# One attention-plus-FFN kernel: the first tiles in another written order, softplus halves side by side once the weights are converted, a chunk's scales computed earlier

## The chip, the cores and the metric

The kernel runs on one core of one Trainium2 chip, in one launch. The metric is the time of an execution in device microseconds (us). It was run three times: median 1319.87 us, lowest 1319.84, highest 1323.7.

## The reference

Two stages follow one another. The first is attention with a threshold, for 8 batches, 8 heads, 576 rows and a head size of 64; the second is a feed-forward network (FFN) with softplus over the 4608 rows that the first gives, 512 wide, with a hidden size of 2048. All inputs are given in 32 bits or more (the two weight matrices come in 64 bits).

```python
scores = scale * np.matmul(q, k.transpose(0, 1, 3, 2))
thresh = np.max(scores, axis=-1, keepdims=True) - tau
scores = np.where(scores >= thresh, scores, -1000000000.0)
attn = np.exp(scores - np.max(scores, axis=-1, keepdims=True))
attn = attn / (np.sum(attn, axis=-1, keepdims=True) + 1e-09)
x = np.matmul(attn, v)           # heads side by side: 4608 x 512
h = x @ w_in                     # 4608 x 2048
g = np.maximum(h, 0.0) + np.log1p(np.exp(-np.abs(h)))
out = g @ w_out                  # 4608 x 512
```

## The kernel before

**Units and tiles.** A unit is one pair of heads of one batch; there are 32. A unit has nine tiles of 128 score rows by 576 columns, so there are 288 tiles in one long row, and the main loop (L1003) goes over them. For tile g the loop writes out, step by step: the row maximum of tile g+2 (`row_max`, VectorE, tile `negm`), its exponentials (`exps`, ScalarE, tile `e_all`, and the threshold `thr`), the mask of tile g+1 (`mask`, VectorE: scores not below the threshold keep their exponential), the f16 high half of the weights of tile g+1 (`weights_hi` L560, GpSimd, tile `h`), the low half of tile g (`weights_lo` L566, VectorE, reads `e_all` and the high half), transposes, some of the FFN's matmuls, and the scores of tile g+3 (`scores` L465, TensorE, tile `s`). There are two PSUM buffers for scores (`banks`, L462): a tile's scores can only be written after the mask two tiles before has read its own. The first five units (`whole`) skip the split in halves and use 32-bit products.

**Halves.** TensorE gets 16-bit operands: a number is split in an f16 high half and an f16 rest. `halves` (L179) does it on GpSimd with two instructions, a conversion (TENSOR_SCALAR) and a subtraction (TENSOR_TENSOR).

**The FFN.** It runs between the tiles, in ten chunks (L893) of 512 or 256 rows. A chunk has 16 blocks `fc` of the hidden size. `hidden` (L699) makes the matmuls of a block into tile `h`, and two blocks at a time (`PAIR`) go through `softplus` (L721): ScalarE writes `st`, then scales it, and its inner function `parts` (L736) has `parts_of` (L747) split each of the two `st` into the halves `g`, with `halves` on GpSimd. `project` (L763) then multiplies `g` by `w_out` into tile `o`, in four quarters `qt` of four blocks for each 128 rows `tb`; `project_out` scales `o` into `acc` on VectorE. At the end of a chunk (`order`, L815) the last pair of blocks waits: `parts` puts itself into `waits` and is let go in the middle of a projection (L779).

**A chunk's scales.** `x_scale` (L654) makes `sx` (two small VectorE instructions) at the last projection ahead of the last quarter of the chunk before (L858). `h_scales` (L665: c0, c1, c2, three instructions of 128x4) and `o_scales` (L676: c3, one) are called from `hidden` (L703) and `project` (L775) at their first use. They are tiles of four numbers a partition.

**What sets the order.** The code is written out once and a scheduler places the instructions; each engine then runs its own queue in order. `defer(n, f)` puts f off by n points (`point`, L877; two points per tile, and the calls at the start), `force` and `need` bring deferred work forward. VectorE, ScalarE and GpSimd instructions go through `Queue` (L149): from tile TQ = 36 on each is tied behind the one written before it, so that these engines run in exactly the written order. Before tile 36 the scheduler is free. `prep` is the list of the weight pieces still to be read and converted, one for every two tiles (L913), 32 in all; it is empty after tile 62.

**The start** (L973 to L1000). Unit 0 is loaded, its K and Q are split (`split_k`, `split_q`: conversion on ScalarE, rest on VectorE for unit 0, on GpSimd for the others) and transposed (`qkT`), all of it for both heads j = 0 and 1, and only then come the scores, row maxima and exponentials of tiles 0 and 1. `queries` (L433) makes for unit 0 a second, swapped copy of the transposed Q with two VectorE instructions (`q` for j = 0, `qT` for j = 1). `plan` (L955) names the tile at which `top_v` (L372, the largest |v| of a unit: `vtop` on VectorE, then a small matmul `topv`) is written.

Of the kernel before, what the change touches and what calls it, by code (L numbers as in the profile page):

```python
# [55 lines left out]
PAIR = 2  # L56
NST = 4
TQ = 36
W1 = 2.0
W0 = 0  # L60
LATE = 4
# [4 lines left out]
def tile_kernel(ctx: ExitStack, tc: tile.TileContext, q, k, v, tau, w_in, w_out, out):  # L66
# [73 lines left out]
    now = {"p": 0, "tile": 0}  # L140
    masked = []

    def behind(i, others):

        if others:
            tc.add_manual_dep(i.ins, others[-1].ins.name, mybir.DependencyInfo(
                mybir.DependencyClass.NoSync, mybir.DependencyReason.DATA), reason="order")

    class Queue:  # L149
# [4 lines left out]
        def __getattr__(self, name):  # L154
            def call(*args, **kwargs):
                i = getattr(self.eng, name)(*args, **kwargs)  # L156
                if now["tile"] >= TQ:
                    behind(i, self.last)
                    self.last = [i]
                return i  # L160
            return call
# [186 lines left out]
    def load_q(s):  # L348
        s.qn = natural(s, q, "qn")
# [13 lines left out]
    def load_v(s):  # L363
        s.vn = apool.tile([P, 10, D], F32, tag="vt" if s.whole else "vn", bufs=2 if s.whole else 1, name=f"vn_{s.i}")
        load_rows(s, s.vn, v)
        for i in range(2):
            nc.sync.dma_start(
                s.vn.rearrange("p (h s) d -> p h s d", h=2)[i * SR:(i + 1) * SR, :, NC, :],
                v[s.b, 2 * s.hp:2 * s.hp + 2, SM:S, :].rearrange("h p d -> p h d"),
            )  # L370
# [29 lines left out]
    def split_q(s, j):  # L400
        t = apool.tile([P, NC + 1, 2 * D], F32R, tag="q2", bufs=1, name=f"q2_{s.i}_{j}")
        z = NC + 1 - j
        qj = s.qn[:, j * (NC + 1):j * (NC + 1) + z, :]
        hi_of(s.eng, t[:, 0:z, 0:D], qj)
        lo_of(s.eng_lo, t[:, 0:z, D:2 * D], qj, t[:, 0:z, 0:D])
        s.q2.append(t)
# [58 lines left out]
    def scores(s, t):  # L465
        if t == 0:
            s.sums = apool.tile([P, 9], F32, tag="sums", name=f"sums_{s.i}")
            s.e, s.sp, s.m, s.e16, s.eT = {}, {}, {}, {}, {}
        sp = banks[nth[0] % SB]
        s.e[t] = e_all[:, nth[0] % EB, :]  # L470
        nth[0] += 1
        s.sp[t] = sp
        if t == M:
            parts = [(qm[:, n, j, :], j) for j in range(2) for n in range(2)]
        else:
            j, c = divmod(t, NC + 1)
            parts = [(s.qT[j][n][:, c * P:(c + 1) * P], j) for n in range(2)]
        for m, (lhs, j) in enumerate(parts):
            for hf in range(2):
                nc.tensor.matmul(sp[:, hf, 0:HS], lhs, s.kT[j][:, hf * HS:(hf + 1) * HS],  # L480
                                 start=(m == 0), stop=(m == len(parts) - 1))

    def row_max(s, t):
        negm = apool.tile([P, 1], F32, tag="negm", bufs=3, name=f"negm_{s.i}_{t}")
        thr = apool.tile([P, 1], F32, tag="thr", bufs=3, name=f"thr_{s.i}_{t}")
        vec.reduce_max(negm, s.sp[t][:, :, 0:HS], axis=AX.XY, negate=True)
        s.m[t] = (negm, thr)
# [156 lines left out]
    def load_x(u, cc):  # L644

        if u.main:
            return
        for b in range(QB):
            need("q", NPAIR * (QB * u.b + b) + cc)
        st = fpool.tile([P, QB * SR], F32, tag="xst", name=f"xst_{u.n}_{cc}")  # L650
        u.st[cc] = st
        nc.sync.dma_start(st, x_d[u.b][:, cc, :])

    def x_scale(u):  # L654
        n = NPAIR * (1 if u.main else QB)
        for i in range(n):
            need("v", n * u.b + i)

        u.sx, u.px = [cpool.tile([P, 1], F32, tag=f"sx{i}", bufs=2, name=f"sx{i}_{u.n}") for i in range(2)]
        u.ch, u.g_top, u.sg, u.co = [cpool.tile([P, NFC // 4], F32, tag=f"c{i}", bufs=2, name=f"c{i}_{u.n}")  # L660
                                     for i in range(4)]
        vec.tensor_reduce(u.sx, v_scale[:, n * u.b:n * (u.b + 1)], axis=AX.X, op=ALU.min)
        inverse(u.px, u.sx)
# [57 lines left out]
    def softplus(u, full):  # L721


        ts, last_ = [], None
        with tc.high_priority(SPP):
            for fc, bank in reversed(full):
                t = fpool.tile([P, TC], F32, tag="st", bufs=NST, name=f"st_{u.n}_{fc}")
                i = act.activation(t, bank, AF.Softplus, scale=u.ch[:, fc // 4:fc // 4 + 1]).ins
                if last_ is not None:
                    tc.add_manual_dep(i, last_.name, mybir.DependencyInfo(  # L730
                        mybir.DependencyClass.NoSync, mybir.DependencyReason.DATA), reason="one table load")
                last_ = i
                ts.append((fc, t))
            for fc, t in reversed(ts):
                act.activation(t, t, AF.Copy, scale=u.sg[:, fc // 4:fc // 4 + 1])
        def parts():  # L736
            if u.n in waits:
                waits[u.n].append(parts)
                return
            for n, (fc, t) in enumerate(reversed(ts)):  # L740
                defer(n, lambda fc=fc, t=t: parts_of(u, fc, t))
        defer(HD[1], parts)

    waits = {}
# [2 lines left out]
    def parts_of(u, fc, t):  # L747

        home, tags, bufs = (fpool, ("gh", "gl"), NG)
        if u.tail:  # L750
            spare = [("kT", "kT", 2), ("qT0", "qT1", 1), ("nat", "nat", 2), ("vt", "vt", 2)]
            i = later_g[0] % (NG + len(spare))
            later_g[0] += 1
            if i >= NG:
                *tags, bufs = spare[i - NG]
                home = apool
        gh, gl = [home.tile([P, TC], F16, tag=tags[i], bufs=bufs, name=f"g{i}_{u.n}_{fc}") for i in range(2)]
        halves(gh, gl, t)
        for i in range(TC // u.T):
            c = slice(i * u.T, (i + 1) * u.T)  # L760
            u.g[fc + i] = (gh[:, c], gl[:, c])
# [49 lines left out]
    nq = NFC // QF  # L811
# [26 lines left out]
    def stream():  # L838
        for cc in range(len(X0), NCC):
            split_x(chunks[0], cc)  # L840
        for it in order():
            u = chunks[it[1]]
            if it[0] == "h":
                yield from hidden(u, it[2])
                continue
            if it[0] == "w":
                waits[u.n] = []
                continue
            if it[4] >= 0:

                nx = chunks[u.n + 1]
                per = NCC * P // u.T
                for cc in range(max(0, (it[4] - 1) * per), min(NCC, it[4] * per)):
                    split_x(nx, cc)
                    if cc + 2 < NCC:
                        load_x(nx, cc + 2)
                if it[4] == 0:
                    x_scale(nx)  # L858
                    load_x(nx, 0)
                    load_x(nx, 1)  # L860
            yield from project(u, it[2], it[3])
            if it[4] >= 0 and it[3] == u.T // P - 1 and (u.n, it[2], it[3]) not in early:
                for cc in range(it[4] * per, NCC):
                    split_x(nx, cc)
# [6 lines left out]
    def defer(n, f):  # L871
        if n == 0:
            f()
        else:
            later.append((now["p"] + n, f))

    def point():  # L877
        now["p"] += 1
        due = [x for x in later if x[0] <= now["p"]]
        later[:] = [x for x in later if x[0] > now["p"]]  # L880
        for _, f in due:
            f()
# [72 lines left out]
    plan = {}  # L955
    for s in units:
        if s.i == 0:
            times = ((0, -1), (0, 0))
        elif s.i == 1:
            times = ((0, -1), (0, 4))  # L960
        elif s.whole:
            times = ((s.i - 1, 4), (s.i - 1, 7))
        else:
            times = ((s.i - 1, 0), (s.i - 1, 3), (s.i - 1, 7))
        for at_, f in zip(times, (load_v, top_v, split_v)):
            plan.setdefault(at_, []).append(lambda f=f, s=s: f(s))
# [11 lines left out]
    eng, u0.eng, u0.eng_lo = u0.eng, act, vec  # L978
    split_k(u0)
    split_q(u0, 0)  # L980
    for n in (0, 2, 1):
        qkT(u0, 0, n)
        point()
    load_v(u0)
    load_k(units[1])
    load_q(units[1])
    split_q(u0, 1)
    for n in (0, 2, 1):
        qkT(u0, 1, n)
        point()  # L990
    u0.eng, u0.eng_lo = eng, pool
    scores(*tiles[0])
    row_max(*tiles[0])
    exps(*tiles[0])
    scores(*tiles[1])
    row_max(*tiles[1])
    exps(*tiles[1])
    mask(*tiles[0])
    scores(*tiles[2])
    load_v(units[1])  # L1000

    done = 0.0
# [81 lines left out]
```

## Time and profile before

The shares are of the span. A line of the profile names an engine, an operation and its operands as output<-inputs, with the buffer numbers left out; L156 stands for every instruction that goes through `Queue`. PE is TensorE's matmuls, PEld its weight loads, DVE is VectorE, ACT is ScalarE, POOL is GpSimd. All times are in us. "idle before <-releaser" is the time for which an engine stood still ahead of an instruction and what ended it.

| | |
|---|---|
| median of three runs | 1319.87 us |
| the profiled execution's own time | 1319.59 us |
| its span (first to last instruction) | 1317.8 us |
| TensorE busy | 1245.7 us (95%) |
| VectorE, ScalarE, GpSimd busy | 936.2, 907.2, 920.2 us |
| largest groups of matmuls | o 407.9, h 360.7 and 229.4, s 152.9 and 107.3, pv 153.6 us |
| mean granted TensorE clock | 0.994 |

Some 1.8 us of the execution lie outside the span.

### The profile page before, as it was taken

What the parts mean: (1) busy time and instruction counts of PE and PEld (TensorE: products, weight loads), DVE (VectorE), ACT (ScalarE), POOL (GpSimd) and SP (SyncE); (2) the same over time, 40 slices, a digit from 0 to 9 for tenths busy, and PEclk for the clock granted to TensorE, in tenths of its full rate; (3) what the DMA queues carried; (4) which work ended last, traced back from release to release, by engine and by line L of the source; (5) the groups of instructions that cost most, each with busy time, mean ns of one, the idle gap of its engine ahead of it and who ended that gap; (6) DMA issues with size and microseconds to landing.
All of it is one profiled execution on the core that took longest, in us unless ns stands there. A gap on an engine that the chain in (4) does not pass through costs nothing.

```text
span 1317.8 us, 21688 instructions
## 1 busy us (share of the span) xinstructions
PE 1245.7 (95%) x7153; PEld 752.0 (57%) x7153; DVE 936.2 (71%) x1738; ACT 907.2 (69%) x1715; POOL 920.2 (70%) x987
## 2 busy tenths in 40 slices
PE   5988988899999999998999899999999999999998
PEld 4655544455566566665666566655656755554455
DVE  5878888988878787888787877886677666640011
ACT  5877887886877677776777697768675867643321
POOL 2577788888777777778877786787666787564333
PEclk9999999999999999999999999999999999999999
DMA  4544458867876678787877787776667665530010
GB/s 127 159 139 126 125 129 165 180 112 149 160 149 146 139 161 152 150 148 161 149 143 145 161 149 142 145 150 132 130 125 163 115 132 114 98 78 17 1 40 17
DMA packets 395521, 168.79 MB, mean 128 GB/s; under 512 B 350448, under 2 KB 376464, under 8 KB 395408
## 3 DMA queue, kind: packets, MB, share of 16 engines
q1 hardware_dynamic: 395408, 167.40, 61.6%
q8 instruction: 57, 0.93, 0.3%
q14 instruction: 56, 0.46, 0.1%
HBM read 56.62 MB, written 10.63 MB: 51 GB/s over the span
## 4 chain that ended last, share of the span: by engine, by line
PE 57%; ACT 15%; POOL 12%; DVE 8%; issue 6%; DMA 2%; SPq 0%; POOLq 0%; ACTq 0%; DVEq 0%
PE o L776 20%; PE h L712 17%; PE s L480 9%; PE pv L591 6%; ACT L156 4%; ACT st L156 4%; POOL g L156 2%; ACT e_all L156 2%; DVE negm L156 2%; PE pv L550 2%; DVE e_all L156 2%; POOL xl L156 2%; PE tr L420 2%; POOL h L156 1%; POOL w_i L156 1%
## 5 line engine op out<-in xcount | busy, mean ns | idle before, releaser
L776 PE MATMUL o<-w_o,g 128*128 128x512 f16 x1728 | 407.9, 382 | 13.9 <-POOL g L156 11.0
L712 PE MATMUL h<-xh,w_i 128*128 128x512 f16 (+1 forms) x1280 | 360.7, 358 | 3.6 <-ACT kT L156 1.9
L156 POOL TENSOR_SCALAR h<-e_all 128x576 f16<-128x576 f32 x243 | 239.3, 985 | 121.5 <-DVE e_all L156 114.9
L156 ACT ACTIVATE e_all<-s,negm 128x576 f32<-128x576 f32 x288 | 213.8, 742 | 132.3 <-DVE negm L156 129.8
L712 PEld LDWEIGHTS <-w_i 128*128 128x128 f16 x1920 | 179.4, 98 | 165.9 <-issue 7.4
L776 PEld LDWEIGHTS <-g 128*128 128x128 f16 x1728 | 159.1, 98 | 191.4 <-POOL g L156 16.3
L156 DVE SCALAR_TENSOR_TENSOR e_all<-s,thr,e_all 128x576 f32<-128x576 f32 x288 | 233.0, 809 | 49.3 <-ACT thr L156 48.8
L156 DVE TENSOR_REDUCE negm<-s 128x1 f32<-128x576 f32 x288 | 215.2, 747 | 73.2 <-PE s L480 72.1
L156 DVE SCALAR_TENSOR_TENSOR h<-e_all,h 128x576 f16<-128x576 f32 x243 | 237.7, 978 | 2.5 <-POOL h L156 2.5
L712 PE MATMUL h<-xl,w_i 128*128 128x512 f16 (+1 forms) x640 | 229.4, 358 | 0.5 <-POOL xl L156 0.5
L156 POOL TENSOR_SCALAR g<-st 128x512 f16<-128x512 f32 x144 | 99.5, 691 | 165.1 <-ACT st L156 156.9
L156 DVE SCALAR_TENSOR_TENSOR acc<-o,c,acc 128x512 f32<-128x512 f32 x108 | 80.2, 743 | 171.8 <-PE o L776 110.6
L156 POOL TENSOR_TENSOR g<-st,g 128x512 f16<-128x512 f32 x144 | 171.2, 1189 | 12.0
L480 PE MATMUL s<-kT,q 128*128 128x288 f32 x768 | 152.9, 328 | 16.1 <-DVE e_all L156 13.6
L156 ACT ACT_TABLE_LOAD x119 | 152.7, 1283 | 3.9 <-DVE negm L156 1.9
L591 PE MATMUL pv<-eT,vt 128*128 128x288 f16 x1080 | 153.6, 288 | 1.2 <-DVE xp L156 0.4
L156 ACT ACTIVATE st<-h,c 128x512 f32<-128x512 f32 x144 | 91.2, 684 | 76.2 <-PE h L712 75.4
L480 PEld LDWEIGHTS s<-kT,q 128*128 128x128 f32 x768 | 115.0, 192 | 49.1 <-DVE e_all L156 35.6
L591 PEld LDWEIGHTS <-vt 128*128 128x128 f16 x1080 | 99.9, 98 | 37.9 <-issue 2.0
L480 PE MATMUL s<-kT,qT 128*128 128x288 f32 x512 | 107.3, 331 | 10.5 <-DVE e_all L156 8.7
L156 ACT COPY xp<-pv 64x288 f32<-64x288 f32 (+3 forms) x133 | 50.7, 385 | 87.1 <-PE pv L591 82.9
L156 ACT ACTIVATE st<-st,c 128x512 f32<-128x512 f32 x144 | 96.3, 716 | 2.3
(113 smaller groups left out, 1512.7 us busy)
## 6 DMA issues: line engine op xcount, KB each, us to landing
q<-q SPq DMA_DIRECT2D x62, 192.0 KB
kn<-in_k_dram SPq DMA_DIRECT2D x32, 256.0 KB
qn<-in_q_dram SPq DMA_DIRECT2D x32, 256.0 KB
vn<-in_v_dram SPq DMA_DIRECT2D x32, 256.0 KB
wc_i<-in_moe_w_in_dram SPq DMA_DIRECT2D x16, 512.0 KB
wc_o<-in_moe_w_out_dram SPq DMA_DIRECT2D x16, 512.0 KB
qT<-qT SPq DMA_DIRECT2D x62, 128.0 KB
out_dram<-acc SPq DMA_DIRECT2D x14, 512.0 KB
```

The costliest lines, as they stand in the source:

```text
L156: i = getattr(self.eng, name)(*args, **kwargs)
L420: nc.tensor.transpose(pr[:, c * P:(c + 1) * P], src, identr)
L480: nc.tensor.matmul(sp[:, hf, 0:HS], lhs, s.kT[j][:, hf * HS:(hf + 1) * HS], start=(m == 0), stop=(m == len(parts) - 1))
L550: nc.tensor.matmul(o[0:D, 0:n], s.vn[k_, 5 * j + c, :], h[k_, c, 0:n], start=(c == 0), stop=(c == NC))
L591: nc.tensor.matmul(o[:, 0:HS], s.vt[:, 5 * j + c, :], s.eT[j][:, c + i, x0:x0 + HS], start=(c == 0 and i == 0), stop=(c == NC and i > 0))
L712: nc.tensor.matmul(bank[:, i * u.T:(i + 1) * u.T], wi[g, cc][:, a, e], x[cc], start=(cc == 0 and m == 0), stop=(cc == NCC - 1 and m == 2))
L776: nc.tensor.matmul(o, u.g[fc][m // 2][:, sl], wo[fc][:, m % 2, :], start=(n == 0), stop=(n == 3 * QF - 1))
```

## The change

There are three parts.

1. **The start.** `Queue` now ties instructions in the written order for tiles 0 to 2 as well (TF = 3), and everything between tile 3 and tile 36 only behind the last of those. In the written order, the transposes of the first head come as n = 0, 1, 2, then the scores, row maxima and exponentials of tiles 0 and 1, and only then the second head's Q and its transposes, with the mask of tile 0 and the scores of tile 2 among them. The second head's Q of unit 0 is split on GpSimd instead of ScalarE and VectorE. `top_v` of units 0 and 1 is written at tiles 4 and 6 in place of 0 and 4.
2. **The halves of a pair.** In `parts`, the second block's halves were put off by one point. They are still put off while `prep` holds work; afterwards both blocks are split one right after the other.
3. **The scales.** `h_scales` and `o_scales` of the next chunk are called right after its `x_scale`.

```diff
--- before.py
+++ after.py
@@ -56,6 +56,7 @@
 PAIR = 2
 NST = 4
 TQ = 36
+TF = 3
 W1 = 2.0
 W0 = 0
 LATE = 4
@@ -154,8 +155,8 @@
         def __getattr__(self, name):
             def call(*args, **kwargs):
                 i = getattr(self.eng, name)(*args, **kwargs)
-                if now["tile"] >= TQ:
-                    behind(i, self.last)
+                behind(i, self.last)
+                if not TF <= now["tile"] < TQ:
                     self.last = [i]
                 return i
             return call
@@ -738,7 +739,7 @@
                 waits[u.n].append(parts)
                 return
             for n, (fc, t) in enumerate(reversed(ts)):
-                defer(n, lambda fc=fc, t=t: parts_of(u, fc, t))
+                defer(n if prep else 0, lambda fc=fc, t=t: parts_of(u, fc, t))
         defer(HD[1], parts)
 
     waits = {}
@@ -856,6 +857,10 @@
                         load_x(nx, cc + 2)
                 if it[4] == 0:
                     x_scale(nx)
+                    need("i", nq - 1)
+                    need("o", nq - 1)
+                    h_scales(nx, 0)
+                    o_scales(nx, 0)
                     load_x(nx, 0)
                     load_x(nx, 1)
             yield from project(u, it[2], it[3])
@@ -955,9 +960,9 @@
     plan = {}
     for s in units:
         if s.i == 0:
-            times = ((0, -1), (0, 0))
+            times = ((0, -1), (0, 4))
         elif s.i == 1:
-            times = ((0, -1), (0, 4))
+            times = ((0, -1), (0, 6))
         elif s.whole:
             times = ((s.i - 1, 4), (s.i - 1, 7))
         else:
@@ -978,25 +983,25 @@
     eng, u0.eng, u0.eng_lo = u0.eng, act, vec
     split_k(u0)
     split_q(u0, 0)
-    for n in (0, 2, 1):
+    for n in (0, 1, 2):
         qkT(u0, 0, n)
         point()
+    u0.eng, u0.eng_lo = eng, pool
     load_v(u0)
     load_k(units[1])
     load_q(units[1])
+    for g in range(2):
+        scores(*tiles[g])
+    for g in range(2):
+        row_max(*tiles[g])
+        exps(*tiles[g])
     split_q(u0, 1)
     for n in (0, 2, 1):
         qkT(u0, 1, n)
         point()
-    u0.eng, u0.eng_lo = eng, pool
-    scores(*tiles[0])
-    row_max(*tiles[0])
-    exps(*tiles[0])
-    scores(*tiles[1])
-    row_max(*tiles[1])
-    exps(*tiles[1])
-    mask(*tiles[0])
-    scores(*tiles[2])
+        if n == 0:
+            mask(*tiles[0])
+            scores(*tiles[2])
     load_v(units[1])
 
     done = 0.0
```

Part 2 on GpSimd, inside chunk 1. Its rows before: `g_1_4` and `g_1_5` are the two blocks of a pair (first the conversion, then the subtraction of each), `h` the high half of a tile's weights, `vt` the halves of v.

```order
L156 TENSOR_SCALAR g_1_4_4136<-st_4_4115 128x512
L156 TENSOR_TENSOR g_1_4_4137<-st_4_4115,g_1_4_4136 128x512
L156 TENSOR_SCALAR h_132<-e_all 128x576
L156 TENSOR_SCALAR g_1_5_4157<-st_5_4113 128x512
L156 TENSOR_TENSOR g_1_5_4158<-st_5_4113,g_1_5_4157 128x512
L156 TENSOR_SCALAR h_132<-e_all 128x576
L156 TENSOR_SCALAR vt_4213<-vn_3883 128x10x64
```

The same place after:

```order
L157 TENSOR_SCALAR g_1_4_4136<-st_4_4116 128x512
L157 TENSOR_TENSOR g_1_4_4137<-st_4_4116,g_1_4_4136 128x512
L157 TENSOR_SCALAR g_1_5_4140<-st_5_4114 128x512
L157 TENSOR_TENSOR g_1_5_4141<-st_5_4114,g_1_5_4140 128x512
L157 TENSOR_SCALAR h_132<-e_all 128x576 x2
L157 TENSOR_SCALAR vt_4213<-vn_3884 128x10x64
```

The conversion of a tile's weights that stood between the two blocks now stands behind them, next to the following tile's. This happens seven times in each of chunks 1 to 4; three of the seven (blocks 4/5, 8/9, 12/13) look like this one, with another `h` next; elsewhere a split of q follows.

Part 2 on GpSimd at the end of chunk 1, where the last pair (blocks 14 and 15) was held back. `xh` and `xl` are the halves of the next chunk's x. Before:

```order
L156 TENSOR_SCALAR g0_1_14_5206<-st_1_14_5173 128x512
L156 TENSOR_TENSOR g1_1_14_5207<-st_1_14_5173,g0_1_14_5206 128x512
L156 TENSOR_SCALAR h16_132<-e_all_129 128x576
L156 TENSOR_SCALAR xh_2_0_5226<-xp_8_3783 128x512
L156 TENSOR_TENSOR xl_2_0_5227<-xp_8_3783,xh_2_0_5226 128x512
L156 TENSOR_SCALAR g0_1_15_5233<-st_1_15_5171 128x512
L156 TENSOR_TENSOR g1_1_15_5234<-st_1_15_5171,g0_1_15_5233 128x512
```

After:

```order
L157 TENSOR_SCALAR g0_1_14_5210<-st_1_14_5177 128x512
L157 TENSOR_TENSOR g1_1_14_5211<-st_1_14_5177,g0_1_14_5210 128x512
L157 TENSOR_SCALAR g0_1_15_5214<-st_1_15_5175 128x512
L157 TENSOR_TENSOR g1_1_15_5215<-st_1_15_5175,g0_1_15_5214 128x512
L157 TENSOR_SCALAR h16_132<-e_all_129 128x576
L157 TENSOR_SCALAR xh_2_0_5234<-xp_8_3787 128x512
L157 TENSOR_TENSOR xl_2_0_5235<-xp_8_3787,xh_2_0_5234 128x512
```

Block 15's halves moved ahead of one `h` and of one x split.

Part 3 on VectorE, at the start of chunk 2. `c0`, `c1`, `c2` are the scales, `xp` takes an attention result out of PSUM, `acc` an FFN result. Before:

```order
L156 TENSOR_REDUCE negm_13_1_5439<-s_0_130 128x1
L156 SCALAR_TENSOR_TENSOR e_all_129,sums_13_5373<-s_1_131,thr_13_0_5400,e_all_129 128x576
L156 SCALAR_TENSOR_TENSOR h16_132<-e_all_129,h16_132 128x576
L156 TENSOR_SCALAR c0_2_5158<-p_i_91,sx1_2_5157 128x4
L156 TENSOR_SCALAR c1_2_5159<-c0_2_5158 128x4
L156 TENSOR_SCALAR c2_2_5160<-c1_2_5159 128x4
L156 TENSOR_TENSOR xp_12_5415<-pv_12_0_5416,xp_12_5415 64x288
L156 SCALAR_TENSOR_TENSOR acc_1_2_4290<-o_1_3_3_5389,c3_1_3528,acc_1_2_4290 128x512
```

After, in the place to which they moved, some 30 rows earlier; the rows above are the same without them:

```order
L157 SCALAR_TENSOR_TENSOR h16_132<-e_all_129,h16_132 128x576
L157 TENSOR_REDUCE sx0_2_5156<-v_scale_90 128x1
L157 TENSOR_SCALAR sx1_2_5157<-sx0_2_5156 128x1
L157 TENSOR_SCALAR c0_2_5158<-p_i_91,sx1_2_5157 128x4
L157 TENSOR_SCALAR c1_2_5159<-c0_2_5158 128x4
L157 TENSOR_SCALAR c2_2_5160<-c1_2_5159 128x4
L157 SCALAR_TENSOR_TENSOR c3_2_5161<-c1_2_5159,p_o_92 128x4
L157 TENSOR_REDUCE negm_12_5_5220<-s_1_131 128x1
```

All four now follow `sx`, ahead of a row maximum. TensorE's order is the same from the middle of chunk 0's last quarter to the end of chunk 5; it differs at the start and at those two chunk ends.

## The prediction

> **What bounds the kernel now.** I read the page first (TensorE is busy for 95% of the span, the others about 70%), then the windows, to see in which stage TensorE stands still. The columns are the window, its length, then busy us of PE, PEld, DVE, ACT and POOL (instructions in brackets), the granted clock, the DMA share and GB/s.
>
> ```profile
> 0.00:25.00 25.00, 11.39 (x53) 9.97 (x54) 13.26 (x27) 12.36 (x27) 6.70 (x15) 1.00 0.59 167
> 25.00:60.00 35.00, 34.28 (x211) 23.60 (x209) 31.16 (x65) 28.61 (x78) 16.09 (x19) 1.00 0.45 129
> 300.00:900.00 600.00, 583.05 (x3412) 355.52 (x3410) 480.40 (x879) 435.15 (x796) 455.71 (x489) 1.00 0.77 150
> ```
>
> TensorE idles 13.6 us in the first 25, under 1 us in the next 35, and 17 us in the 600 of the steady stage. In that stage it is the bound: an idle microsecond taken from it is a microsecond off the time, if nothing else takes its place. The waits of TensorE, with their total, count and longest, say what it stood still for:
>
> ```profile
> PE o L776 <- POOL g L156: 11.0, 12, 1.9
> PE tr L413 <- DVE xp L156: 4.3, 6, 1.2
> ```
>
> These two kinds stand at chunk ends and chunk starts, and parts 2 and 3 of the change move just the instructions that they wait for. The start is the third place.
>
> **Part 2, the gain at the chunk ends.** The end of chunk 2, first TensorE, then GpSimd (start, duration, engine, instruction, and in brackets the idle time before it with its releaser):
>
> ```profile
> 591.94 1.69 PE L776 MATMUL o<-w_o,g 128*128 128x512 f16 x7
> 595.53 0.82 PE L776 MATMUL o<-w_o,g 128*128 128x512 f16 x3 [1.91 <-POOL g L156]
> 596.77 0.60 PE L776 MATMUL o<-w_o,g 128*128 128x512 f16 x2 [0.42 <-POOL g L156]
> ```
>
> ```profile
> 588.87 1.17 POOL L156 TENSOR_TENSOR g<-st,g 128x512 f16<-128x512 f32 x1
> 590.00 0.68 POOL L156 TENSOR_SCALAR h<-e_all 128x576 f16<-128x576 f32 x1
> 592.65 0.62 POOL L156 TENSOR_SCALAR xh<-xp 128x512 f16<-128x512 f32 x1 [1.97 <-ACT xp L156]
> 594.86 0.62 POOL L156 TENSOR_SCALAR g<-st 128x512 f16<-128x512 f32 x1
> 595.56 1.15 POOL L156 TENSOR_TENSOR g<-st,g 128x512 f16<-128x512 f32 x1
> ```
>
> TensorE is out of operands at 591.94 + 1.69 = 593.6 and waits for the last block's conversion (594.86) and subtraction (595.56). These sit behind an h and an x split, and that split waits 1.97 for ScalarE. Written next to the first block, they start at 590.0 and end at 590.0 + 0.62 + 0.08 + 1.15 = 591.9, 1.7 us before TensorE needs them; the 1.97 of idle takes them in, so x is not late. Both waits go, 2.33 us here. The row of waits has all twelve of this kind at 11.0, and each is a last block, so I take 11.0. What is late next: the four score matmuls after it need a mask that stands ahead of the `weights_lo` of 592.74 (quoted below) on VectorE and so had ended by then, and the next projection's operands are long there. Nothing is seen to take the place.
>
> **Part 2, the cost between the tiles.** The same edit puts the conversion of a tile's weights behind a pair instead of between its blocks, 28 times in chunks 1 to 4. VectorE needs it for `weights_lo`. GpSimd, VectorE and TensorE at one of them:
>
> ```profile
> 396.86 0.67 POOL L156 TENSOR_SCALAR h<-e_all 128x576 f16<-128x576 f32 x1
> 398.20 1.16 POOL L156 TENSOR_TENSOR g<-st,g 128x512 f16<-128x512 f32 x1
> 399.33 1.17 POOL L156 TENSOR_SCALAR h<-e_all 128x576 f16<-128x576 f32 x1
> ```
>
> ```profile
> 399.04 0.93 DVE L156 SCALAR_TENSOR_TENSOR h<-e_all,h 128x576 f16<-128x576 f32 x1
> 400.01 0.76 DVE L156 TENSOR_REDUCE negm<-s 128x1 f32<-128x576 f32 x1
> 400.68 0.81 DVE L156 SCALAR_TENSOR_TENSOR e_all<-s,thr,e_all 128x576 f32<-128x576 f32 x1
> ```
>
> ```profile
> 401.58 0.87 PE L480 MATMUL s<-kT,q 128*128 128x288 f32 x4
> ```
>
> VectorE goes without a gap from `weights_lo` (399.04) over the row maximum to the mask, which ends at 401.49, and TensorE's scores follow 0.09 later. A `weights_lo` that ends later is thus paid by TensorE. After the change the h of 396.86 ends where the pair ends now, at 398.20 + 1.16 = 399.36, and the next h, whose mask is done, runs right behind it to about 400.03. How VectorE fares beside a running GpSimd conversion is seen at the chunk end, where `weights_lo` starts 0.09 after the xh of 592.65 above; the second row is one without company:
>
> ```profile
> 592.74 1.14 DVE L156 SCALAR_TENSOR_TENSOR h<-e_all,h 128x576 f16<-128x576 f32 x1
> 587.39 0.75 DVE L156 SCALAR_TENSOR_TENSOR h<-e_all,h 128x576 f16<-128x576 f32 x1
> ```
>
> It takes 1.14 in place of 0.75 and ends 593.88, 0.61 after xh's end (593.27). By that, `weights_lo` would end at 400.03 + 0.61 = 400.64 instead of 399.97: 0.67 later, less the 0.09 of slack, 0.58. I take 0.55 a place. It applies at the three places a chunk where another h follows the pair, 12 in chunks 1 to 4, so 6.6 us. Where a split of q follows I take nothing; that is an assumption, since those 16 places are not shown, and rival (c) prices its failure. One more place, in chunk 0, where a weight subtraction follows h, I put at 0.5, like the others. The bounds for a place are 0 (VectorE takes its turn before the second h) and 0.7.
>
> The Trainium skill speaks against this part of the change: "SBUF — State Buffer", section "Who interferes with whom", says that a VectorE instruction with two SBUF inputs contends with a GpSimd instruction that reads SBUF, and that whoever issues first keeps the shared port for its whole instruction. By it `weights_lo` would run its full 0.75 after 400.03, 0.81 late at 12 places, 9.7 us in place of 6.6, and the result would be about 1314. The pair of rows 592.65 and 592.74 agrees with the wait, but shows 0.61 and not 0.75 behind it.
>
> **Part 3, the scales.** At the start of chunk 3, VectorE, then TensorE, then VectorE at the place to which the scales move (end of chunk 2), and the group of c3:
>
> ```profile
> 611.79 0.63 DVE L156 TENSOR_SCALAR c<-p_i,sx 128x4 f32<-128x4 f32 x1
> ...
> 612.74 0.44 DVE L156 TENSOR_TENSOR xp<-pv,xp 64x288 f32<-64x288 f32 x1
> ```
>
> ```profile
> 613.24 0.28 PE L413 MATMUL tr<-identr,k 128*128 128x128 f32 x1 [1.10 <-DVE xp L156]
> ```
>
> ```profile
> 585.24 0.15 DVE L156 TENSOR_SCALAR sx<-sx 128x1 uint32<-128x1 uint32 x1
> 585.99 0.76 DVE L156 TENSOR_REDUCE negm<-s 128x1 f32<-128x576 f32 x1 [0.60 <-PE s L480]
> 586.66 0.81 DVE L156 SCALAR_TENSOR_TENSOR e_all<-s,thr,e_all 128x576 f32<-128x576 f32 x1
> ...
> L156 DVE SCALAR_TENSOR_TENSOR c<-c,p_o 128x4 f32<-128x4 f32 (+1 forms) x13 | 7.6, 587 | 0.0
> ```
>
> ```profile
> 589.52 0.88 PE L480 MATMUL s<-kT,qT 128*128 128x288 f32 x4
> ```
>
> A transpose of TensorE waits 1.10 for a PSUM buffer that xp frees, and the three scales ahead of xp take 612.74 - 611.79 = 0.95. Without them xp starts 0.95 sooner and 0.15 of the wait stays. Of the 4.3 us of such waits I take 3.8. In the new place the four cost 0.95 + 0.59 = 1.5, of which 0.6 fall in the idle time before the row maximum. The mask after it then ends near 588.4 instead of 587.5; the scores that need it start at 589.52, so this is hidden, by a margin of 1.1.
>
> **Part 1, the start.** VectorE and TensorE:
>
> ```profile
> 11.13 0.82 DVE L156 TENSOR_REDUCE vtop<-vn 128x1 f32<-128x640 f32 x1 [1.60 <-DMA vn<-in_v_dram]
> 11.97 1.51 DVE L156 TENSOR_SCALAR q<-tr,qscale 64x512 fp32r<-64x512 f32 x2
> ...
> 16.70 1.51 DVE L156 TENSOR_SCALAR qT<-tr,qscale 64x512 fp32r<-64x512 f32 x2 [0.45 <-ACT qT L156]
> 18.25 0.82 DVE L156 SCALAR_TENSOR_TENSOR e_all<-s,thr,e_all 128x576 f32<-128x576 f32 x1
> ...
> 18.99 0.81 DVE L156 SCALAR_TENSOR_TENSOR e_all<-s,thr,e_all 128x576 f32<-128x576 f32 x1
> ```
>
> ```profile
> 13.54 1.09 PE L480 MATMUL s<-kT,q 128*128 128x288 f32 x3 [2.02 <-DVE q L156]
> 19.13 1.33 PE L480 MATMUL s<-kT,q 128*128 128x288 f32 x4 [3.67 <-DVE e_all L156]
> ...
> 21.18 1.31 PE L480 MATMUL s<-kT,q 128*128 128x288 f32 x4
> ```
>
> The copy q (11.97) waits behind a vtop that waits for v's transfer; without it q can start sooner by the 1.60 of that wait or a little more, near 10.0 (an estimate), and tile 0's scores end some 1.5 us sooner. Tile 0's mask (18.25) then goes ahead of qT and ends, by my estimate, near 15.7, not 19.0. But qT's 1.51 and a row maximum of 0.76 now stand before tile 1's mask, and qT, whose operands come from the second head's split, is put at no earlier than 17.0 (an estimate: now it starts at 16.70, and its split is written later): that mask begins at 17.0 + 1.51 + 0.76 = 19.2, as it does now (18.99). Tile 3's scores wait for it and start at 20.0, not at 21.18. So the first 25 us give back 1.1 us of the 3.67 and 2.02. Against this, two vtop (0.82 each) and three weight conversions of ScalarE move into the window 25:60, where TensorE is busy 34.28 of 35 and VectorE 31.16; VectorE would be at 32.8 there. I take 1.0, and from -1 to +3 as bounds.
>
> **The sum.** 11.0 + 3.8 + 1.0 - 6.6 - 0.5 = 8.7 us. From the profiled execution's own 1319.59 that gives 1310.9; the median of the runs is 0.28 above it, hence 1311.
>
> **The rivals.**
>
> (a) The moved conversions cost nothing: VectorE gets its turn between two h, or TensorE makes up for it at the next scores. For it: the shared stretch now already holds `weights_lo` up (0.93 at 399.04). Against it: the two h run without a gap on GpSimd. Then the gain is 15.8 - 0.5 = 15.3 and the time 1304.6.
>
> (b) The time won at the chunk ends is lost again: VectorE's masks run nearly back to back after a chunk's end, and if they set the pace there, half of the 11.0 stays. Then 8.7 - 5.5 = 3.2, 1316.7, no change to speak of. Against it: in the 600 us of the steady stage VectorE is busy for 480.40, so it stands idle for a fifth of it, seven times as long as TensorE.
>
> (c) Slower: each of the 28 moved conversions holds VectorE up by 0.65, not only the 12, because a split of q that runs on GpSimd holds it just as an h does. 28 x 0.65 = 18.2 against 15.3 gives +2.9, 1322.8. It decides from 15.3 / 28 = 0.55 a place on. For it: the 0.61 row is a conversion of the same kind as a q split. Against it: the 28 places are then all without slack on VectorE, which is idle for a fifth of this stage.
>
> (d) The clock. Two windows, with the clock in the third column from the end:
>
> ```profile
> 400.00:500.00 100.00, 97.20 (x562) 59.10 (x561) 81.58 (x149) 69.44 (x128) 75.07 (x81) 0.98 0.71 150
> 500.00:600.00 100.00, 97.63 (x577) 59.62 (x576) 78.10 (x148) 72.39 (x135) 73.39 (x81) 1.00 0.80 147
> ```
>
> The first lost 2% of its clock, 2 us, and holds a chunk end; the second holds one too and lost none. If it was that wait, removing it gives 2 us more, 1309; I do not count on it. The Trainium skill, "TensorE: Matmul & The Clock Gate", section "Part 1: The HAM clock gate", has TensorE fall to half its clock after about 3.4 us of idling; no wait in these windows is as long.
>
> **How the numbers follow.** About 0.3%, 4 us, can be told from no change here. Chances: the forecast 0.54, with 1307 to 1315 as its own bounds; (a) 0.16; (b) 0.14; (c) 0.07; (d) 0.09. Faster by over 0.3%, below 1315.9: the forecast, (a) and (d), 0.79. Within: (b), 0.14. Slower: (c), 0.07. The range from 1303 to 1317 holds all but (c) and the ends of (a) and (b): its low end is (a) with a start better by 1.6, its high end (b).
>
> **What would show it.** In the profile after: the waits of o for g near zero in place of 11.0, and of tr for xp below 1; h, h and `weights_lo` at the 12 places with `weights_lo` above 1 us or starting some 0.4 later, and scores of TensorE that wait about 0.5 for a mask there; tile 3's scores at about 20. I am wrong if the waits for g stay, if TensorE shows no new waits for masks between 330 and 890 (then it is (a)), or if the window 25:60 idles more than the start wins.

## The result and the profile after

The changed kernel took 1308.27 us (median of 4 runs, 1307.21 to 1309.13) where the kernel before took 1319.86: a ratio of 0.9905, interval 0.9885 to 0.9926. That is 11.6 us off, which here and below means so many us less; the forecast was 8.7 off, 1311, with a range of 1303 to 1317. The time by itself does not tell the forecast (1307 to 1315) from rival (d), 1309. The profiled execution took 1309.13, its span 1307.4, 10.4 less than before.

The windows of the changed kernel, with the columns as before:

```profile
0.00:25.00 25.00, 12.72 (x56) 11.06 (x57) 10.77 (x21) 10.11 (x23) 5.98 (x14) 1.00 0.60 167
25.00:60.00 35.00, 34.37 (x197) 22.69 (x196) 32.31 (x68) 27.96 (x74) 15.54 (x20) 1.00 0.39 112
300.00:900.00 600.00, 592.51 (x3499) 364.73 (x3497) 487.82 (x897) 447.84 (x821) 463.13 (x503) 1.00 0.78 153
```

TensorE now idles 7.5 us in the 600 of the steady stage, not 17. Of its waits, o for g and (but for one of 0.2) the transposes of L414 for xp are gone from the list; three rows of the list tell what there is instead (scores for a mask were 22.4 before, pv for xp 0.4, and the small matmul topv had no row):

```profile
PE s L481 <- DVE e_all L157: 23.5, 28, 2.2
PE pv L592 <- DVE xp L157: 2.0, 4, 0.5
PE topv L379 <- DVE xp L157: 1.5, 2, 1.0
```

The two waits of topv stand at the ends of chunks 0 and 5. The forecast had none there. They come with the scales: 1.2 in the trace of the scales alone, and no such row in that of the halves alone.

The end of chunk 2, TensorE first, then GpSimd, then TensorE at the start of chunk 3:

```profile
591.33 2.77 PE L777 MATMUL o<-w_o,g 128*128 128x512 f16 x12
593.93 0.39 PE L379 MATMUL topv<-identr,vtop 128*128 128x128 f32 x2
```

```profile
589.78 0.61 POOL L157 TENSOR_SCALAR g<-st 128x512 f16<-128x512 f32 x1
590.48 1.16 POOL L157 TENSOR_TENSOR g<-st,g 128x512 f16<-128x512 f32 x1
591.60 0.67 POOL L157 TENSOR_SCALAR h<-e_all 128x576 f16<-128x576 f32 x1
```

```profile
608.61 0.32 PE L414 MATMUL tr<-identr,k 128*128 128x128 f32 x1
```

The last block's subtraction ends at 591.64, the twelve matmuls run in one piece, and the transpose at 608.61 waits for nothing. One piece also saves more than the idle time: 7 + 3 + 2 matmuls took 1.69 + 0.82 + 0.60 = 3.11 before, 12 in a row take 2.77. By this place, each cut costs 0.17 beside the wait that the profile names.

To see where the rest went, I set the row maxima of the two traces side by side: the n-th VectorE row `negm<-s` is tile n's. How much later it starts after the change (us, minus is sooner):

```
tile            0      4     16     32     72     84    112    120    148    156    184    192    220    228    256    284
before      14.42  25.56  58.68 113.88 289.71 339.63  444.2  478.3  583.0  616.5  721.1  754.7  859.3  893.5 1017.2 1144.8
difference  -1.98  -0.92  +1.84  +3.20  +3.03  +2.68  +3.32  -1.24  -0.61  -4.65  -3.98  -7.99  -7.35 -10.87 -11.61 -10.71
```

| stretch | forecast | measured |
|---|---|---|
| start, to tile 16 | -1.0 | +1.84 |
| tiles 16 to 72 | 0 | +1.2 |
| end of chunk 0, tiles 72 to 84 | about -1.6 | -0.35 |
| ends of chunks 1 to 5 | about -12.8 | -16.9 (4.56 + 4.04 + 4.01 + 3.52 + 0.74) |
| inside chunks 1 to 4 | +6.6 | +2.6 (0.64 + 0.63 + 0.67 + 0.64) |
| after tile 256 | 0 | +0.9 |

So the chunk ends gave more, the moved conversions cost less, and the start lost where a gain was forecast. The experiments take these in turn. Each kernel was timed beside the kernel before on one chip, and each gain below is taken from the latter's median there: 1320.8 in the first set of four, 1320.1 in the second, 1322.0 in the third (three kernels) and 1320.9 beside the last.

### The profile page after: what moved, and what is told of

The parts are those of the page before. It is cut to its first block, busy times and chain, and to the rows that moved or that the text cites. A ratio compares the mean times of both kernels' runs of the same rounds, so it can differ in the third digit from the quotient of the medians.

```text
span 1307.4 us, 21708 instructions
## 1 busy us (share of the span) xinstructions
PE 1246.2 (95%) x7153; PEld 755.2 (58%) x7153; DVE 932.5 (71%) x1737; ACT 905.5 (69%) x1714; POOL 914.8 (70%) x989
## 4 chain that ended last, share of the span: by engine, by line
PE 48%; ACT 16%; DVE 13%; POOL 10%; issue 7%; DMA 4%; SPq 1%; DVEq 0%; POOLq 0%; ACTq 0%
PE o L777 16%; PE h L713 15%; PE s L481 8%; PE pv L592 6%; ACT st L157 5%; ACT L157 4%; POOL g L157 4%; DVE e_all L157 3%; DVE negm L157 3%; ACT e_all L157 2%; DVE h L157 2%; PE pv L551 1%; POOL h L157 1%; DVE wa_i L157 1%; POOL w_i L157 1%
## 5 line engine op out<-in xcount | busy, mean ns | idle before, releaser
L157 POOL TENSOR_SCALAR h<-e_all 128x576 f16<-128x576 f32 x243 | 229.0, 945 | 114.8 <-DVE e_all L157 108.7
```

## Experiments: each part by itself

**The start alone.** The two other parts are taken out of the changed kernel:

```diff
-                defer(n if prep else 0, lambda fc=fc, t=t: parts_of(u, fc, t))
+                defer(n, lambda fc=fc, t=t: parts_of(u, fc, t))
...
-                    need("i", nq - 1)
-                    need("o", nq - 1)
-                    h_scales(nx, 0)
-                    o_scales(nx, 0)
```

> Before with part 1 alone (the start). Theory A, that the start itself loses: tile 3's scores come about 1.8 us earlier than before (near 19.4), but TensorE's matmuls are still at the slow rate (128x288 x4 in 1.3 us, not 0.8) until about 27.7 instead of 24, so the row maximum of tile 16 comes about 1.8 later than before; total +1.8, near 1321.7. Rival B, the forecast: the start gains 1, near 1318.9, and what the changed kernel lost in its first 120 us was the chance place of half-speed spells.

Measured: 1321.63, ratio 1.0011, 1.0000 to 1.0023. In its trace tile 4's row maximum is 0.91 sooner than before and tile 16's 1.52 later, as in the changed kernel. The interval just reaches 1, so it is the row maxima that show the loss: in the six traces with the old start and no extra products, tile 16 lies between 1.01 sooner and 0.13 later than in the kernel before. The start loses by itself; the rival, that a gain of 1 was only covered by chance, falls.

**The halves alone** (the diff's one line in `parts`, on the kernel before).

> Before with part 2 alone. Theory A: four chunk ends give 2.67 each (the two waits of 2.33 and 0.34 of restarting), ends of chunks 0 and 5 some 1.0 together; the moved conversions cost 0.65 a chunk (0.49 and 0.34 of new waits, less 0.17 that goes), 2.6 in all: 11.7 - 2.6 = 9.1 off, near 1310.8. Rival (the forecast's loss of 0.55 at 12 places, 6.6): near 1314.8. Rival (no loss at all): near 1308.2. If a half-speed spell near 458 goes with the wait there, each is 1.7 lower.

Measured: 1314.92, ratio 0.9953 (0.9941 to 0.9964): 5.9 off, where theory A had 9.1. A row of its waits shows what A had missed:

```profile
PE tr L413 <- DVE xp L156: 8.3, 6, 1.8
```

Before, the row read 4.3 in all. The waits for xp at the chunk starts (1.10 at 613.24 before) grow to 1.68: part of what the chunk end wins comes back at the next chunk start, behind the same three small instructions. From tile 148 to 156 this kernel wins 2.10.

**The scales alone** (the diff's four lines after `x_scale`, on the kernel before).

> Before with part 3 alone. Theory A: the transposes at the starts of chunks 1 to 5 no longer wait for xp (1.15, 0.17, 1.10, 1.08, 0.65, and up to 0.26 of restarting each): 4 to 5 off, near 1315.4. Rival: the four small instructions hold up a mask in their new place and a wait of TensorE's scores for e_all of the same size appears there: no change, 1319.9.

Measured: 1315.18, ratio 0.9955 (0.9942 to 0.9968), 5.6 off. The waits of tr for xp are gone (but for some of 0.1 to 0.2), and of those for g the eight at the ends of chunks 1 to 4 stay, as this row of the waits says; the four short ones at the ends of chunks 0 and 5 are gone. No new wait for a mask of that size is there at the chunk ends, but the two of topv for xp are (0.69 and 0.53). Tiles 148 to 156 win 0.99.

```profile
PE o L776 <- POOL g L156: 9.3, 8, 1.9
```

**Both, with the old start.**

> Parts 2 and 3 with the old start. By the drift of the row maxima in the changed kernel's trace, chunk ends 1 to 5 give 15.2 and the stretches inside chunks 1 to 4 take 2.6 back, chunk 0 gives 0 to 1.3 and the end takes 0.9: 11.7 to 13 off the kernel before. Theory A (the start costs 1.8, the two gains need each other): 12 to 13 off, 1 to 2 better than the changed kernel was. Rival (the gains of the two parts add up as measured alone, 5.9 + 5.6): 11.5 off.

Measured: 1308.75 (1305.72 to 1310.08), ratio 0.9906 (0.9890 to 0.9922), 11.4 off. In the traces the two parts do need each other: tiles 148 to 156 win 4.05 together, 2.10 + 0.99 = 3.09 apart. The times don't show it: 11.4 is what the two add up to (5.9 + 5.6), and the start's loss does not show in them either (the changed kernel was 11.6 off). Runs of one kernel differ by 4 here, so the medians leave both open.

## Experiments: the moved conversions

A first try changed nothing of what it meant to. It let only those pairs lie side by side that had put themselves into `waits`:

```diff
-                waits[u.n].append(parts)
+                waits[u.n].append(lambda: parts(1))
...
-                defer(n, lambda fc=fc, t=t: parts_of(u, fc, t))
+                defer(0 if held else n, lambda fc=fc, t=t: parts_of(u, fc, t))
```

> Before with part 3, and of part 2 only the pair that is held back to a chunk's end; between the tiles the halves stay apart, and the start is the old one. Theory A: the chunk-end gain and the scales' gain come without the 2.6 of the moved conversions and without the start's 1.8: 11.7 + 4.5 = 16.2 off, near 1303.7, and the new waits of pv for xp (0.49) and of scores for e_all (0.34) are not there. Rival: these waits come from the chunk end being shorter, not from the moved conversions, and stay: near 1306.3.

Measured: 1314.24, ratio 0.9955 (0.9942 to 0.9968), as the scales alone. Its instructions are those of the scales alone, in the same order on every engine; only in chunk 7 does the edit touch a pair, and there it moves nothing. In chunks 0 to 6 the last pair reaches `parts` after the list has been emptied. What I wrote of `waits` ahead of the prediction is thus true of chunk 7 only; elsewhere the last pair is late because its matmuls are written just ahead of that projection. The kernel stands as a second measurement of the scales alone. The edit that does it asks for the block number:

```diff
-                defer(n, lambda fc=fc, t=t: parts_of(u, fc, t))
+                defer(0 if full[-1][0] >= NFC - PAIR and not prep else n, lambda fc=fc, t=t: parts_of(u, fc, t))
```

> Old start, part 3, and of part 2 only the last pair of a chunk (blocks 14 and 15) split side by side; all other pairs stay apart. Theory A: the chunk ends give all they gave, and the waits of pv for xp (0.49) and of scores for e_all (0.34) inside the chunks are gone, since no conversion of weights moves there: 2.6 better than parts 2 and 3 whole, 15 off the kernel before. Rival: these waits belong to the shorter chunk end and stay: the same as parts 2 and 3 whole, 12 to 13 off.

Measured: 1302.25 (1300.35 to 1304.79), ratio 0.9862 (0.9845 to 0.9880), 17.9 off and 6.5 better than parts 2 and 3 whole. This is the best kernel of the study. Against the run with both parts whole, its row maxima gain 3.0 from tile 84 to tile 228, 0.6 to 0.8 in each of chunks 1 to 4, 1.67 in chunk 0 at tiles 72 to 76, and 0.7 from tile 228 to tile 284; the rest, 1.1, is within what runs differ by. So most of the +0.9 after tile 256 goes with the halves as well: pairs behind chunk 4 moved too, and at tiles 272 to 274 the three traces with the halves whole lose 0.7 to 1.3, this one and that of the scales alone nothing. What the moved conversions do shows in the changed kernel's trace. GpSimd, VectorE and TensorE at blocks 4 and 5 of chunk 3 (640.69 before):

```profile
637.79 1.30 POOL L157 TENSOR_SCALAR h<-e_all 128x576 f16<-128x576 f32 x2
```

```profile
637.18 0.82 DVE L157 SCALAR_TENSOR_TENSOR e_all<-s,thr,e_all 128x576 f32<-128x576 f32 x1 [1.78 <-ACT thr L157]
...
638.49 1.21 DVE L157 SCALAR_TENSOR_TENSOR h<-e_all,h 128x576 f16<-128x576 f32 x1 [0.49 <-POOL h L157]
...
640.29 0.80 DVE L157 SCALAR_TENSOR_TENSOR e_all<-s,thr,e_all 128x576 f32<-128x576 f32 x1
```

The `weights_lo` among them (638.49) before the change:

```profile
642.57 1.24 DVE L156 SCALAR_TENSOR_TENSOR h<-e_all,h 128x576 f16<-128x576 f32 x1
```

TensorE after it:

```profile
641.15 0.80 PE L481 MATMUL s<-kT,q 128*128 128x288 f32 x4 [0.34 <-DVE e_all L157]
```

And at blocks 8 and 9 (673.74 before):

```profile
672.33 1.21 DVE L157 SCALAR_TENSOR_TENSOR h<-e_all,h 128x576 f16<-128x576 f32 x1 [0.26 <-POOL h L157]
...
674.13 0.80 DVE L157 SCALAR_TENSOR_TENSOR e_all<-s,thr,e_all 128x576 f32<-128x576 f32 x1
```

```profile
672.76 2.12 PE L777 MATMUL o<-w_o,g 128*128 128x512 f16 x9
674.99 0.79 PE L481 MATMUL s<-kT,q 128*128 128x288 f32 x4
```

`weights_lo` waits and runs long at both, as forecast: at the first it ends at 639.70, and by its old place (642.57 + 1.24 = 643.81, and this stretch now runs 4.66 sooner) it would have ended at 639.15, so it is 0.55 late. It ends 0.61 behind the second conversion (637.79 + 1.30 = 639.09), the figure taken in the forecast; by the rule of the Trainium skill that was weighed there ("SBUF — State Buffer", "Who interferes with whom") it would be a full 0.75: the row bears out the wait, and not the 0.75. But only at the first does TensorE pay much, 0.34. At the second the mask ends near 674.9 and TensorE is busy with nine matmuls of a projection until 672.76 + 2.12 = 674.88, so it idles 0.1; at the third (blocks 12 and 13) it is 0.1 too. The other cost is at blocks 0 and 1, where a split of q follows and the forecast took nothing:

```profile
621.71 0.99 DVE L157 SCALAR_TENSOR_TENSOR h<-e_all,h 128x576 f16<-128x576 f32 x1 [0.86 <-POOL h L157]
622.73 0.46 DVE L157 TENSOR_TENSOR xp<-pv,xp 64x288 f32<-64x288 f32 x1
```

```profile
623.25 1.39 PE L592 MATMUL pv<-eT,vt 128*128 128x288 f16 x10 [0.49 <-DVE xp L157]
```

`weights_lo` waits 0.86 for the conversion, the xp behind it comes late, and pv waits for that. With the conversions back in their places none of these waits is in the trace (only 0.16 at one set of scores per chunk, which the kernel before has too).

## Experiments: the start

TensorE in the changed kernel (scores of tiles 2, 3 and 4, products pv of tile 0, scores of tile 5; the transposes between them are left out), then tile 4's scores in the kernel before:

```profile
15.07 1.33 PE L481 MATMUL s<-kT,q 128*128 128x288 f32 x4 [2.19 <-DVE e_all L157]
...
19.40 1.33 PE L481 MATMUL s<-kT,q 128*128 128x288 f32 x4 [1.93 <-DVE e_all L157]
...
22.31 2.29 PE L481 MATMUL s<-kT,q 128*128 128x288 f32 x8 [0.52 <-DVE e_all L157]
...
26.06 1.72 PE L551 MATMUL pv<-gw,vn 128*64 128x256 f32 x4
27.71 0.80 PE L481 MATMUL s<-kT,qT 128*128 128x288 f32 x4
```

```profile
24.07 1.37 PE L480 MATMUL s<-kT,q 128*128 128x288 f32 x8
```

Tile 3's scores come at 19.40, 1.78 sooner than before, even better than the 20.0 of the forecast. But four matmuls take 1.33 up to here and 0.80 from 27.71 on. In the kernel before, the eight of tile 4 at 24.07 take 1.37 and not 2.29, so TensorE was at the full rate from there: 3.6 sooner. None of this shows as idle time: in the window from 25 to 60 TensorE is 34.37 busy, before 34.28. The work between was done at half rate. The other traces agree: tile 4's eight take 1.32 to 1.50 near 24 in all six with the old start and no extra products, and 2.29 in that of the start alone. There the full rate was reached once, at tile 2, and was gone again at tile 3:

```profile
15.08 0.80 PE L481 MATMUL s<-kT,q 128*128 128x288 f32 x4 [2.19 <-DVE e_all L157]
...
19.41 1.33 PE L481 MATMUL s<-kT,q 128*128 128x288 f32 x4 [2.88 <-DVE e_all L157]
```

The first try to test that put products of the identity in the start, into a PSUM tile that nobody reads:

```diff
+    def warm(n):
+        ps = ps_g.tile([P, 512], F32, tag="g", name="warm")
+        for _ in range(n):
+            nc.tensor.matmul(ps[:, 0:P], ident, ident, start=True, stop=True)
...
+    warm(36)
```

with 10 and 8 more among the first tiles.

> The changed kernel with 54 extra 128x128 products of the identity by itself (36 before the first data arrive, 18 among the first tiles, into a PSUM tile that nobody reads). Theory A, the start is slow because TensorE runs its matmuls at half rate until 27.7: with TensorE kept busy the 128x288 x4 groups take 0.8 and not 1.33 from the first tile on, and the row maximum of tile 16 comes 2.5 to 4 sooner: near 14.5 off the kernel before. Rival, the loss is in the order of the scheduler (row maximum and pv ahead of tile 5's scores): the groups may get shorter, but tile 16 stays within 1 of the changed kernel's 60.5: 11 to 12 off.

> The kernel before with the same 54 extra products. Theory A: it was already at full rate from 24.1 on, so it wins less than the changed kernel does: 1 to 2 off. Rival: it wins as much as the changed kernel, 3 or more, since its chain of the first four tiles is just as slow.

Measured: 1312.18 (ratio 0.9938, 0.9924 to 0.9953) and 1326.62 (1.0050, 1.0036 to 1.0064), both slower than without. The size was wrong: each product is two matmuls, in the changed kernel the first 36 end at 11.8, and the first transposes, which could start at 6.6, wait behind them; in the kernel before ScalarE's copy kT then came late as well, a wait of 4.39. The first of the two traces tells two things. TensorE does reach the full rate early by this (first row), and it loses it again over a wait of 3.39 (second):

```profile
18.14 0.80 PE L481 MATMUL s<-kT,q 128*128 128x288 f32 x4
...
23.28 1.33 PE L481 MATMUL s<-kT,q 128*128 128x288 f32 x4 [3.39 <-DVE e_all L157]
```

Smaller numbers (13 ahead of the data, a few behind tile 1's and tile 2's scores) gave no clear answer:

> The changed kernel with extra products of the identity by itself again, sized by the run before this one (72 matmuls took 9.68 and pushed everything back by 5): 13 products that end before the first data arrive (6.6), 4 behind tile 1's scores and 5 behind tile 2's, each into the idle time there. Theory A, half-rate matmuls until 27.7 are what the start lost by: groups of four 128x288 take 0.8 from the first scores on, no idle of TensorE above 2, and the row maximum of tile 16 is at 57.0 to 58.5, 2 to 3.5 sooner than in the changed kernel (60.5) and no later than in the kernel before (58.7): 13.5 to 15 off. Rival, the order of the scheduler: the groups take 0.8, but tile 16 stays at 60 or later, and the time at 11 to 12 off.

> The old start with the last pair alone side by side and the early scales (17.9 off the kernel before), and extra products of the identity: 13 ahead of the first data, 10 behind tile 1's scores. Theory A: TensorE is at the full rate from the first scores on, where it was at half rate until 24; tile 16's row maximum 1 to 2 sooner than 58.6, 19 to 20 off. Rival: the chain over VectorE and ScalarE sets the first four tiles, and full rate alone gives less than 0.5.

> The changed kernel's start, the early scales, only the last pair side by side, and the extra products as in the first run of this set. It should be the first run of this set less the cost of the moved conversions (3.0 in chunks 1 to 4 and 1.7 in chunk 0 by the two traces with the old start): 4.7 better than it, 18 to 19.5 off the kernel before; if the starts with full rate differ, it tells which of the two is better by comparison with the run before it.

Measured: 1308.86 (0.9911, 0.9892 to 0.9931), 1306.61 (0.9887, 0.9873 to 0.9902) and 1304.48 (0.9870, 0.9855 to 0.9886). All three missed their totals. The third was forecast 4.7 better than the first and is 4.4 better, a second measurement of what the moved conversions cost; of the start they tell nothing. With the extra matmuls the scheduler wrote the second head's transposes behind tile 2's scores, in the old start it let ScalarE's copy kT come so late that TensorE stood still for 7.43, and in the changed one the half rate was back after a wait of 3.39 before tile 3's scores. The last run therefore tied each extra product behind the instruction that ends ahead of an idle stretch, and reordered nothing else:

```diff
+    def fill(n, ps, i):
+        for _ in range(n):
+            j = nc.tensor.matmul(ps, ident, ident, start=True, stop=True)
+            behind(j, [i])
+            i = j
...
```

> The changed kernel with 13 extra products of the identity in the three stretches of its start in which TensorE idled: 5 behind tile 1's scores (12.9 to 15.1), 6 behind tile 0's transposes (17.5 to 19.4), 2 behind tile 1's; nothing else is reordered, on no engine. Theory A, what the new start loses is that TensorE stays at half rate until 27.7 because it idles in between: it is at full rate by 20, tile 4's eight score matmuls take 1.35 and not 2.29, tile 5's scores start near 25.9 and not at 27.7, and the row maximum of tile 16 is near 58.7, 1.8 sooner than in the changed kernel: the loss of the start is gone. Rival, the order after tile 3 (a row maximum ahead of the mask, pv ahead of tile 5's scores) costs it by itself: the groups get shorter, but tile 16 stays at 60 or later. The whole time can move by 1.8 at most, beside runs that differ by more than that; tile 16 decides.

Measured: 1307.05, ratio 0.9896 (0.9879 to 0.9913). TensorE, at the same places as above:

```profile
14.62 0.81 PE L489 MATMUL s<-kT,q 128*128 128x288 f32 x4 [0.94 <-DVE e_all L157]
...
18.95 0.79 PE L489 MATMUL s<-kT,q 128*128 128x288 f32 x4 [1.64 <-DVE e_all L157]
...
21.33 1.32 PE L489 MATMUL s<-kT,q 128*128 128x288 f32 x8 [0.59 <-DVE e_all L157]
...
23.41 1.08 PE L562 MATMUL pv<-gw,vn 128*64 128x256 f32 x4
24.42 0.80 PE L489 MATMUL s<-kT,qT 128*128 128x288 f32 x4
```

Tile 5's scores start 3.3 sooner than in the changed kernel, and tile 16's row maximum is at 58.0, 2.55 sooner (0.44 of it was there at tile 0, ahead of the extra products). It is 0.7 sooner than in the kernel before. All other instructions come in the order of the changed kernel on every engine, so the order by itself is not what costs. With the half rate gone the new start wins about what the forecast gave it up to tile 16; the half rate is what it lost by. The whole times (ratios 0.9896 and 0.9905) are too close to show it.

## Why the prediction was right, point by point

**Chunk ends (+11.0) and scales (+3.8): right, a little small.** Every wait went as written. At the ends of chunks 1 to 4 none took its place, as forecast; at those of chunks 0 and 5 the 1.5 of topv did, which the forecast did not see. The stretches at the ends of chunks 1 to 5 gave 16.9. 1.7 of it is a half-speed spell (next point), and some 2 are, by the figure of chunk 2, the cuts: about a dozen waits gone, 0.17 each. Chunk 0's end gave 0.35 in place of 1.6: the conversions moved there cost 1.67, not the 0.5 that I gave them. What the forecast did not see is that the two terms depend on each other: without the scales, 0.6 of each chunk end is given back at the next chunk start.

**The clock, rival (d): borne out by a count.** In the kernel before a spell at half the granted clock (third column from the end) begins near 457.7, between the ends of the two waits at 456.8 and 458.0, and ends near 461.1:

```profile
457.00:457.50 0.50, 0.50 (x3) 0.10 (x1) 0.00 (x0) 0.00 (x0) 0.50 (x1) 1.00 0.89 124
457.50:458.00 0.50, 0.12 (x1) 0.00 (x0) 0.00 (x0) 0.00 (x0) 0.50 (x2) 0.68 0.73 136
458.00:458.50 0.50, 0.46 (x2) 0.19 (x3) 0.00 (x0) 0.00 (x0) 0.50 (x1) 0.50 0.97 184
...
461.00:461.50 0.50, 0.50 (x3) 0.20 (x2) 0.50 (x2) 0.15 (x1) 0.50 (x1) 0.90 0.00 0
```

In the five traces of kernels that have the waits of o for g, such spells stand at 7 of the 20 ends of chunks 1 to 4. In the nine traces without these waits, with either start, there is none after 300 us until the last matmuls. 7 / 20 of 4 ends at 1.7 each (half of 3.4) make 2.4 us an execution (an estimate) that would belong to the change; that the waits call the spells is a count, not a proof, since no run put one wait back alone. I had leaned against (d) on the Trainium skill's word ("TensorE: Matmul & The Clock Gate", "Part 1: The HAM clock gate") that about 3.4 us of idling are needed. The spells here are 3.4 long, but the waits beside them are of 1.9 and 0.4; the measurement decides. Spells before tile 72 (in the window from 100 to 125 the changed kernel lost 12% of its clock, the kernel before 4%) fell differently in each run; they are most of the +1.2 between tiles 16 and 72, and no step of the change was found for them.

**Moved conversions (-6.6): the mechanism right, the price wrong.** `weights_lo` is 0.55 late, as worked out. The step that failed is "a `weights_lo` that ends later is thus paid by TensorE": at one place of three it is (0.34), at the others TensorE has queued work to run until the mask is all but done and pays 0.1. The assumption that the other 16 places cost nothing failed at four of them (0.49). Together 2.6 to 3.0 in chunks 1 to 4. The moves behind chunk 4, which the forecast left out, add 0.7 at tiles 272 to 274. Rivals (a), no cost, and (c), 18.2, are both off.

**The start (+1.0): wrong in sign.** By the time of the run with the start alone (0.8 lost) it lies inside the bounds of -1 to +3, by tile 16 (1.84 and 1.52 lost) outside. The order and tile 3's scores came as written. The step that failed is reading the start in idle time alone: the first 25 us do hold less idle time (12.72 busy in place of 11.39, 1.3 against the 1.1 forecast), but I took the durations of the old trace, and in the new order TensorE comes to the full rate 3.6 later.

**Rival (b), gains lost again at the chunk ends,** is not seen in the changed kernel. Where the scales stay (halves alone) 0.6 of each end is lost again, but behind xp and not behind the masks.

**The sum.** That it came within 2.9 is in part luck. By the table, the chunk ends 1 to 5 gave 4.1 more than forecast and the conversions in chunks 1 to 4 cost 4.0 less, while the start, the stretch to tile 72, chunk 0 and the end together were 6.2 worse.

## What to carry to other kernels

A stage where an engine is busy all the time can still be slow: compare the duration of the same instruction early and late before an idle time is turned into a gain. When work is moved to close a gap at one place, apply the rule to that place alone: the last pair of a chunk needed it, and the seven others a chunk paid for it; the kernel with that pair alone, the early scales and the old start (0.9862) beats both parts whole (0.9906) and the changed kernel (0.9905). And two waits in a row on one path hide each other: by the traces, a part measured alone can be worth less than with its partner (3.09 and 4.05 at one chunk end), though the times here did not show it.

## What was not expected of the hardware

In the kernel before and the changed one the granted clock of the profile stays at 1.00 in the first 25 us, though the same matmuls take 1.33 there and 0.80 later; the half rate of the start shows in durations only. After a wait of 3.39 behind a stretch at the full rate TensorE was back at half rate, in three runs, and after waits of 2.19 and 2.88 in that of the start alone. An interrupted run of 128x512 matmuls cost 0.17 more at each cut than its idle time says, at the one place where it was compared.
